# First batch's q and k turned by unit-matrix products, last batch in two token parts, and a new order of work

## The chip, the cores and the metric

The kernel runs on one core of one Trainium2 chip. The metric is the device time of one execution in microseconds (us); the time before is the median of three runs.

## The reference

Two stages follow each other. All inputs are float32.

```python
# stage 1: window attention, B=8, H=8, S=576, D=64, window 32 on both sides
scores = (q @ k.T) / 8                       # per batch and head
scores = where(|i - j| <= 32, scores, -1e9)
x = softmax(scores) @ v                      # heads side by side: x is [8, 576, 512]

# stage 2: four attention experts (E=4, width 64), two chosen per token
logits = x @ w_gate                          # [8, 576, 4]
w = softmax over the two largest logits of a token
for e in range(4):
    q, k, v = x @ wq[e], x @ wk[e], x @ wv[e]
    ye = softmax(causal(q @ k.T / 8)) @ v @ wo[e]
    out += (weight of e for the token, or 0) * ye
```

## The kernel before, in words

The work is cut into short steps, and the string `ORDER` lists some nine hundred of them by name. The program is built by walking the list: every step appends its instructions to the queues of the engines that it uses, and each engine works through its own queue in that order. So the list, written out as a constant, fixes what each engine does next. A step is written as `op`, `batch`, further digits, then a letter for the engine or the queue (`a` ScalarE, `v` VectorE, `g` GpSimd; for loads `e` SyncE's queue and `f` ScalarE's queue), then `@` and the banks of PSUM. PSUM has eight banks, all in one tile `PS`; a step that writes a bank waits until the bank's last reader is done.

A load (`load`) also waits for the last TensorE instruction ahead of it in the list, and all but one of the loads and all stores of the kernel before go through the queue of SyncE. A step of TensorE that stands late in the list thus holds the loads behind it.

The steps of the window attention of a batch, where a batch's eight heads are two groups of four:

- `lq`, `lk`, `lv`: loads of q, k and v. A group's q or k is 128 rows (four heads, 32 positions each) of 18 x 64 elements; a load of part 0 is all of it, 576 KB, and parts 1 and 2 are its halves.
- `tq`, `tk` (line 292): VectorE turns 32x32 blocks, two instructions for each group and each of q and k, one for each half of the 64 elements of a head (`dh`). They give `Tqn` and `Tkn`.
- `sc` (line 177 through the helper `mm`): the scores. A batch's group has two halves of 288 columns. A half is ten blocks, five for each `dh`, each over four heads, so 40 products that contract 32 rows and accumulate over `dh`.
- `ex` (line 337): ScalarE's exponential out of PSUM, two instructions for a half. `mk` (line 341): the window mask as a product, on GpSimd or VectorE.
- `vc`: a copy of v to other partitions. `av`: probabilities times v, in five pieces of the tokens. `un` (lines 368 to 374): the division by the row sum on VectorE.
- `xt` (line 180): TensorE transposes the result; `xf` and `xb` (lines 169 and 171, the helper `copy`) bring it out of PSUM and into bf16.

The steps of the experts, where four experts are two pairs `j`: `ga`, `gt`, `ge`, `gm`, `gu` for the gate; `pp`/`pe` for the projections; `pv`/`ve` for the values; `ps`/`xe`/`se` for scores, exponential and causal mask; `po` for probabilities times values of a pair, `oe` (lines 552 to 554) for its division; then the pair is turned, by a DMA (`dt`, line 567) in batches 0 to 6 and on TensorE (`pt`, copied out by `ot`) in batch 7; `py`, `ye`, `st` for the output projection, its copy and its store.

At the start, `zz` steps run four products of a zero matrix each. Their results are never read. The constants are made by the `s_` steps; `s_pads` writes the fixed zeros and ones of several tiles on VectorE.

Of the kernel before, what the change touches and what calls it, by code (L numbers as in the profile page):

```python
# [8 lines left out]
F32 = mybir.dt.float32  # L9
# [10 lines left out]
S = 576  # L20
# [4 lines left out]
NOE = 4  # L25

ORDER = """
    s_zero s_ones lk000:e lq000:e lv03 lk012:e tk000:e lq011:f zz1@0 zz0@0 lq012:e lk011:e s_ident s_mask lq100:e
    tq000:e sc000@02 lk100:e s_warm ex0001@2 tq011:e ex0000@0 sc001@46 ex0010@4 lv01 lv02 zz4@0 tk012:e tq012:e
    tk011:e sc010@02 mk0001:g mk0000:v ex0100@0 tq100:e lv00 tk100:e ex0101@2 zz2@4 lk110:e sc011@40 ex0011@6 zz3@2  # L30
    ex0110@4 mk0011:g vc00:a lv04 s_pads lq110:e lw00 sc101@26 vc01:a mk0101:v mk0100:v lw11 ex0111@0 av01@4 un01@4
    mk0110:g mk0010:g mk0111:g av00@0 un00@0 av04@4 lw2 xt00@0 un04@4 xf00:a@0 av03@4 ex1010@2 ex1011@6 tk110:e lw01
    av02@0 lq200:e un03@4 sc100@26 lk200:e xt02@4 ex1001@6 xf02:a@4 un02@0 xt01@0 xb02:a tq110:e mk1011:g sc110@64
    ex1000@2 xb00:g cw11:g xf01:v@0 lw10 tq200:e cw01:g mk1000:g cw2:g sc111@20 ex1101@4 xb01:a cw10:g lv13 lv11
    pp011@4 ex1100@6 lwg cw00:a tk200:e pp010@6 lv12 lv10 ex1110@2 pp000@2 pe011:a@4 pe000:v@2 pp001@4 ex1111@0
    sc201@02 lq210:e pe001:v@4 pe010:a@6 ps002@6 mk1010:v ga0@4 mk1111:v mk1110:v mk1100:v lv14 mk1101:g mk1001:g
    vc10:g ex2010@0 vc11:g lk210:e gt0@4 ps001@0 xe002@6 se002 ex2011@2 xe001@0 pv00@6 sc200@20 lq300:e tq210:e
    ve00:a@6 ex2000@2 av12@6 un12@6 ex2001@0 ps011@2 xe011@2 lq310:e ge0@4 av13@0 un13@0 ps000@2 pv01@5 xe000@2 av10@6
    tk210:e ps03@0 lv21 un10@6 xt11@2 ve01:a@5 xe03@0 av11@0 xf11:a@2 lk300:e un11@0 lv22 av14@5 ps010@2 un14@5 gm0@4
    xt10@6 xf10:v@6 xe010@2 xt12@5 xf12:a@5 sc211@02 lv20 lv24 tq300:e lv23 xb12:a ex2110@0 ga1@5 gt1@5 gu0@4 sc210@60  # L40
    ex2111@2 xb11:a mk2010:g mk2000:g se010 mk2011:g xb10:g lq400:e mk2001:g pp110@2 ex2100@6 ex2101@0 pp101@6 ge1@5
    tk300:e pp111@0 pe110:a@2 pe101:a@6 vc20:a mk2111:g mk2101:g se011 lw3 lk310:e pe111:v@0 gm1@5 gu1@5 tq310:e
    mk2100:g vc21:g pp100@2 pe100:a@2 pv11@4 sc300@60 mk2110:g ex3000@6 ex3001@0 pv10@2 ve10:a@2 av21@6 lq410:e av23@0
    un21@6 av22@2 un23@0 ps101@6 un22@2 lv32 ps100@0 av24@5 cw3:g se000 mk3000:g se001 xe100@0 xe101@6 se03 un24@5
    xt21@2 lv31 xt22@5 lk400:e xf22:v@5 xf21:a@2 ve11:v@4 xb22:g ps012@0 av20@6 sc301@24 un20@6 xt20@6 xe012@0
    ex3011@4 lv33 tk310:e ex3010@2 mk3001:g xb21:g se012 xf20:a@6 po00@0 lq500:e ps13@4 ps112@2 po01@6 xe112@2 oe00@0
    xe13@4 ps102@0 xe102@0 sc311@24 oe01@6 mk3011:g mk3010:g ex3111@4 lk500:e xb20:g sc310@60 pp201@4 ex3110@2 lv30
    lk410:e ex3100@6 ex3101@0 ps111@2 ps110@6 pp200@0 pe201:a@4 tk400:e xe111@2 lv34 pp211@4 tq400:e pp210@2 xe110@6
    lv42 pe210:a@2 pe200:v@0 pe211:v@4 tq410:e pv20@6 ve20:a@6 sc400@02 mk3101:g mk3111:g mk3100:g vc31:g se101
    mk3110:g dt00 se100 vc30:g tk410:e dt01 ex4000@0 ex4001@2 lv40 sc401@46 ps202@0 ga2@2 ex4011@6 mk4011:g se110 se13  # L50
    mk4001:g se102 lv43 pv21@3 av33@6 lq600:e xe202@0 av30@0 ve21:a@3 ex4010@4 gt2@2 py02@3 ge2@2 ye02:a@3 lk600:e
    av32@4 gm2@2 un33@6 un30@0 av34@3 py01@6 lv41 ye01:a@6 gu2@2 un32@4 un34@3 po10@0 xt32@2 lv50 xf32:a@2 av31@4
    ps23@6 xe23@6 oe10@0 ps211@2 un31@4 xe211@2 xt31@0 ps210@6 mk4000:g xe210@6 sc411@42 xf31:v@0 lv51 lq510:e xt30@0
    ex4110@4 ex4111@2 tk500:e tq500:e xf30:a@0 sc410@64 ex4101@4 py00@2 ye00:v@2 ex4100@6 se112 xb32:g mk4010:g se111
    xb31:g ps201@0 vc41:g ps200@4 xb30:g se202 vc40:g pp301@6 xe201@0 xe200@4 pp311@0 lk510:e pe301:v@6 sc501@24
    pe311:a@0 sc500@60 ex5010@2 tq510:e lv44 pp300@2 ex5011@4 lv53 ex5000@6 pp310@4 po11@6 ex5001@0 pe300:a@2 tk600:e
    pe310:a@4 oe11@6 ps300@0 ps301@2 mk4101:g mk4110:g mk4111:g av43@4 se200 mk4100:g lk610:e pv31@6 xe300@0 av40@0
    xe301@2 av41@2 un43@4 un40@0 ve31:a@6 lv54 av42@4 un41@2 ps212@6 dt10 ps302@0 xe212@6 ga3@2 xe302@0 av44@3 un42@4
    ps33@4 xe33@4 tq600:e dt11 un44@3 st00 xt41@6 xf41:a@6 lv61 lv52 xt40@0 gt3@2 ge3@2 gm3@2 xt42@3 xf40:a@0 xf42:a@3
    sc600@46 ex6001@6 ex6000@4 mk5000:g lq610:e tk510:e mk5010:g se201 se300 se210 se302 xb41:g se212 se23 se211  # L60
    xb42:a pv30@0 gu3@2 lv63 ve30:v@0 xb40:a sc510@64 mk5011:g ex5100@6 lv64 lq710:e pp401@2 pe401:a@2 pp411@0
    pe411:a@0 po20@6 oe20@6 st02 st01 ex5101@4 py10@2 ye10:a@2 st10 sc511@04 sc601@62 ex5111@4 lk710:e ex5110@0
    ex6011@2 po21@4 ps310@0 ex6010@6 tk610:e oe21@4 tq610:e se33 ps312@2 pp410@6 xe310@0 xe312@2 vc50:g mk6000:g
    mk5100:g mk5001:g vc51:g mk5101:g pe410:a@6 se301 pp400@0 pe400:a@0 po30@4 mk5111:g se310 lq700:e ps311@2 oe30@4
# [12 lines left out]
    pp610@2 lv74 se502 pp601@4 pe610:v@2 mk7100:g po50@0 xe511@6 se511 mk7110:g ps611@2 pe601:v@4 ps602@6 xe611@2
    oe50@0 po41@4 xe602@6 oe41@4 ps610@0 av71@2 xe610@0 av70@6 un71@2 ps600@4 ps510@0 dt41 xe510@0 un70@6 av72@2
    xe600@4 av73@6 ps612@0 xe612@0 ps601@4 un72@2 av74@2 un73@6 st30 ga6@3 un74@2 ps63@6 ps512@0 xe601@4 gt6@3 xe63@6
    xt71@4 ge6@3 xe512@0 se510 se600 se612 se512 xt72@2 xf71:a@4 py31@6 gm6@3 gu6@3 se611 dt40 py40@0 xt70@4 xf72:a@2  # L80
    xb72:g ye40:a@0 xb71:g po51@2 ye31:v@6 py32@0 oe51@2 xf70:a@4 py42@1 pv71@4 pv61@5 st31 st40 py41@6 dt51 xb70:g
    se602 se63 pv60@2 ye41:a@6 ve60:v@2 se610 se601 ve71:v@4 pv70@6 ve61:a@5 dt50 po61@2 ve70:a@6 pp710@4 po60@6
    ye32:v@0 st32 oe61@2 st41 pp711@2 pe710:a@4 oe60@6 pe711:a@2 pp701@4 ye42:v@1 ps710@6 pe701:a@4 ps712@0 xe712@0
    py50@2 ye50:v@2 pp700@4 xe710@6 py51@0 pe700:a@4 ps73@6 ps711@2 xe73@6 st42 se73 se710 se712 xe711@2 ps701@4 dt60
    ye51:v@0 xe701@4 ga7@6 gt7@6 ps702@0 xe702@0 se701 ps700@2 dt61 st50 se711 py52@7 ge7@6 xe700@2 ye52:v@7 py60@4
    gm7@6 se702 po71@0 gu7@6 st51 py61@2 oe71@0 se700 po70@6 pt71@0 oe70@6 st52 ye60:a@4 ot71:v@0 st60 py62@1 pt70@4
    ot70:v@4 ye61:a@2 st61 py701@0 py710@2 ye701:v@0 py700@3 ye62:a@1 st62 st701 py72@0 ye710:v@2 py711@1 ye700:a@3
    st710 ye711:a@1 st700 st711 ye72:v@0 st72
# [559 lines left out]
```

## Time and profile before

| | us |
|---|---|
| median of 3 runs | 236.77 (235.77 to 236.83) |
| the profiled execution's own time | 235.27 |
| its span, first to last instruction | 233.5 |
| TensorE (PE) busy | 213.4 (91% of the span) |
| VectorE (DVE) busy | 180.2 (77%) |
| GpSimd (POOL) busy | 148.9 (64%) |
| ScalarE (ACT) busy | 146.3 (63%) |
| granted TensorE clock, mean | 0.995 |

Busy time is the union of an engine's instructions in the trace. Every TensorE product of float32 stands in the trace as two records, and the end of a record is modelled, so an engine that is called busy may still be waiting for a part of that time. "PEld" is TensorE's loading of the stationary matrix, which overlaps its products. An instruction's idle time before it carries the name of what released it; "issue" means that the profile shows nothing that it waited for.

### The profile page before, as it was taken

The numbers are of one execution on the slowest core, as the hardware profiler recorded it, in microseconds if no ns is written. First come the engines' busy times: TensorE is split into PE (matmuls) and PEld (weight loads), VectorE is DVE, ScalarE is ACT, GpSimd is POOL, SyncE is SP. The second block draws the span as 40 slices with busy tenths as digits, with TensorE's granted clock in tenths as the row PEclk, the third lists the DMA queues.
The fourth block names the chain that finished last, engine by engine and source line by source line (L and its number), as shares of the span: only waits on it lengthen the run. The fifth ranks groups of instructions, "written<-read, shape, count | busy, mean of one in ns | idle before, by whom it ended". The sixth has DMA issues, their size and how long they took to land.

```text
span 233.5 us, 12227 instructions
## 1 busy us (share of the span) xinstructions
PE 213.4 (91%) x5472; PEld 169.7 (73%) x5486; DVE 180.2 (77%) x354; ACT 146.3 (63%) x223; POOL 148.9 (64%) x180
## 2 busy tenths in 40 slices
PE   6497999989999999899999969999999999999970
PEld 1374877868798977786898758987788787786540
DVE  1998889999977996779889449998577477645671
ACT  2067356856756876368768558577686667746931
POOL 7028195754996876989957598398978662630500
PEclk9999999999999999999999999999999999999998
DMA  6988889867867789956669975696752016284865
GB/s 234 317 207 237 208 253 207 247 207 194 212 210 202 235 261 113 247 151 149 170 151 157 280 272 188 156 81 170 171 152 93 6 25 150 101 139 137 251 213 204
DMA packets 64549, 42.94 MB, mean 184 GB/s; under 512 B 54768, under 2 KB 55792, under 8 KB 64496
## 3 DMA queue, kind: packets, MB, share of 16 engines
q1 hardware_dynamic: 64352, 41.86, 70.0%
q8 instruction: 43, 0.70, 1.3%
q10 hardware_dynamic: 144, 0.29, 0.4%
q14 instruction: 10, 0.08, 0.1%
HBM read 30.42 MB, written 9.44 MB: 171 GB/s over the span
## 4 chain that ended last, share of the span: by engine, by line
PE 59%; DVE 19%; POOL 7%; DMA 7%; issue 5%; ACT 1%; DVEq 0%; POOLq 0%; ACTq 0%
PE PS L177 55%; DVE Tkn L292 6%; DVE Tqn L292 4%; PE PS L180 4%; DVE A L341 3%; DMA V<-in_v_dram 3%; POOL A L341 3%; POOL V L171 2%; DMA kn<-in_k_dram 2%; DVE XN L369 2%; DMA out_dram<-Y 2%; POOL XTB L171 1%; POOL ATE L517 1%; DVE XTF L171 1%; DVE RC L368 0%
## 5 line engine op out<-in xcount | busy, mean ns | idle before, releaser
L341 POOL TENSOR_TENSOR A<-A,MASKP 128x576 f32<-128x576 f32 x57 | 80.0, 1416 | 20.0 <-ACT A L337 19.6
L514 ACT ACTIVATE ATE<-PS 128x1024 bf16<-128x1024 f32 x48 | 47.3, 1024 | 16.5 <-PE PS L177 14.0
L337 ACT ACTIVATE A<-PS 128x576 f32<-128x576 f32 x64 | 38.9, 651 | 23.7 <-PE PS L177 22.7
L177 PE MATMUL PS<-Tqn,Tkn 32*64 32x128 f32 (+3 forms) x2560 | 46.4, 276 | 6.8 <-DVE Tqn L292 4.6
L177 PEld LDWEIGHTS PS<-Tqn,Tkn 32*64 32x64 f32 x2560 | 40.4, 135 | 15.2 <-DVE Tqn L292 6.3
L177 PE MATMUL PS<-V,A 128*64 128x65 f32 (+1 forms) x1280 | 40.8, 223 | 3.4 <-DVE XN L369 1.2
L177 PEld LDWEIGHTS PS<-V,A 128*64 128x64 f32 (+1 forms) x1280 | 36.9, 132 | 7.9 <-issue 3.0
L292 DVE STREAM_TRANSPOSE Tkn<-kn 128x576 f32<-128x576 f32 (+1 forms) x34 | 37.4, 1180 | 6.4 <-DMA kn<-in_k_dram 5.6
L517 POOL TENSOR_SCALAR_AFFINE_SELECT ATE<-ATE 128x256 bf16<-128x256 bf16 x64 | 25.6, 414 | 24.7 <-ACT ATE L514 20.7
L292 DVE STREAM_TRANSPOSE Tqn<-qn 128x576 f32<-128x576 f32 (+1 forms) x34 | 37.2, 1178 | 0.6 <-DMA qn<-in_q_dram 0.6
L171 POOL COPY V<-V 64x2048 f32<-64x2048 f32 (+1 forms) x12 | 21.0, 1748 | 6.3 <-DMA qn<-in_q_dram 2.8
L369 DVE TENSOR_TENSOR XN<-PS,RC 128x512 f32<-128x512 f32 x32 | 22.1, 692 | 1.2
L177 PE MATMUL PS<-WO,OTT 128*128 128x512 bf16 (+1 forms) x85 | 18.4, 342 | 1.5 <-DVE OTT L171 0.8
L180 PE MATMUL PS<-ident,XN 128*128 128x128 f32 x144 | 19.1, 278 | 0.0
L169 ACT COPY XTF<-PS 128x128 f32<-128x128 f32 (+1 forms) x23 | 13.6, 631 | 7.6 <-PE PS L180 6.9
L177 PE MATMUL PS<-XTB,WK 128*128 128x288 bf16 x128 | 17.9, 286 | 0.4 <-issue 0.3
L177 PE MATMUL PS<-WV,XTB 128*128 128x256 bf16 (+1 forms) x192 | 18.2, 256 | 0.0
L169 ACT COPY Y<-PS 128x1024 f32<-128x1024 f32 (+2 forms) x13 | 9.8, 752 | 13.2 <-PE PS L177 13.2
L177 PE MATMUL PS<-XTB,WQ 128*128 128x288 bf16 x128 | 17.9, 286 | 0.0
L169 ACT CAST QKE<-PS 128x576 bf16<-128x576 f32 x21 | 13.4, 645 | 6.8 <-PE PS L177 6.8
L177 PEld LDWEIGHTS <-ATE 128*128 128x128 bf16 x448 | 16.1, 97 | 2.0 <-issue 0.4
L171 DVE COPY Y<-PS 128x1024 f32<-128x1024 f32 (+2 forms) x13 | 11.6, 894 | 7.5 <-PE PS L177 4.4
(76 smaller groups left out, 273.0 us busy)
## 6 DMA issues: line engine op xcount, KB each, us to landing
kn<-in_k_dram SPq DMA_DIRECT2D x15, 576.0 KB, 4.8
qn<-in_q_dram SPq DMA_DIRECT2D x15, 576.0 KB, 5.1
V<-in_v_dram SPq DMA_DIRECT2D x32, 256.0 KB, 4.2
out_dram<-Y SPq DMA_DIRECT2D x14, 512.0 KB, 4.0
V<-in_v_dram SPq DMA_DIRECT2D x8, 128.0 KB, 4.6
out_dram<-Y SPq DMA_DIRECT2D x16, 64.0 KB, 2.9
out_dram<-Y SPq DMA_DIRECT2D x4, 256.0 KB, 2.6
kn<-in_k_dram SPq DMA_DIRECT2D x2, 288.0 KB, 5.7
```

The lines of the kernel that those rows point to most:

```text
L169: nc.scalar.copy(o, i)
L171: eng(c).tensor_copy(o, i)
L177: last_pe[0] = nc.tensor.matmul(*a, **kw)
L180: last_pe[0] = nc.tensor.transpose(*a)
L292: nc.vector.transpose(T[:, :].rearrange("q (p o) -> q o p", o=18)[:, o0:o1], n_[:, o0:o1, 32 * dh:32 * dh + 32])
L337: nc.scalar.activation(AT[(2 * b + g) % NAT_][half][p], two(b0)[:, :, 0:HS], EXP, scale=scale_att)
L341: eng(c).tensor_tensor(out=ap, in0=ap, in1=MASK[:, None, HS * half:HS * half + HS].to_broadcast([128, 2, HS]), op=MULT)
L369: nc.vector.tensor_tensor(out=XN[T // 2][:, T % 2, :].rearrange("p (g h d) -> p g h d", g=2, h=4), in0=u[:, :, :, 0:64], in1=rc[:, :, :, N ...
L514: nc.scalar.activation(chunk(ATE[(2 * b + j) % len(ATE)], ch), two(b0), EXP, scale=scale_moe)
L517: nc.gpsimd.affine_select(ap, ap, pattern=[[0, n], [1, w]], compare_op=IS_GE, fill=0.0, base=0, channel_multiplier=-1)
```

## The change

Three things change.

1. In batch 0 both groups' q and k are no longer turned on VectorE. New steps `hq`, `hk` and `hr` multiply 64-row slices of the loaded tile by a 64x64 unit matrix on TensorE, 32 products in `hq` and in `hk` (16 of a head's 18 slices for two halves of the partitions) and 8 in `hr` (the last two slices of q and of k). New steps `eq`, `ek` and `er` copy the results out of PSUM into `QKT`. These hold a whole head's 64 elements on 64 partitions, so `sc` of batch 0 contracts 64 rows at once: 20 products for a half where there were 40. The loads of batch 0 are no longer cut into halves.
2. In batch 7, `po`, `oe`, `pt` and `ot` of each pair are each cut in two by tokens: tiles 0 and 1, and tiles 2 to 4. One store of the last batch goes through ScalarE's queue.
3. `ORDER` is another list. Over the whole list, VectorE has 7 masks before and 10 after, of 64; of the 26 steps `ye` it has 13 before and 7 after, of the 24 steps `xf` 7 and 4, of the 32 steps `pe` 11 and 13; what leaves it goes to ScalarE, but the masks come from GpSimd. ScalarE also takes four of the six weight conversions `cw` where it had one.

```diff
-    QKT = {nm: [many(2, [128, S], F32, f"T{nm}{g}") for g in range(2)] for nm in ("qn", "kn")}
+    QKT = {nm: many(2, [128, 2, S], F32, f"T{nm}") for nm in ("qn", "kn")}
...
+    PETURN = ((0, 0), (0, 1))
+
+    def turn_rows(nm, b, g, todo):
+        n_ = NAT[nm][(2 * b + g) % NNAT]
+        for r, o, bank, at in todo:
+            s = slice(64 * r, 64 * r + 64)
+            mm(PS[s, bank, at:at + 64], n_[s, o, :], ident[s, s], start=True, stop=True, skip_group_check=True)
+
+    def turn16(nm, b, g, b0):
+        turn_rows(nm, b, g, [(r, 8 * (u ^ r) + i, b0 + (u ^ r), 64 * i)
+                             for u in range(2) for i in range(8) for r in range(2)])
...
+    def hr(c, b, g, b0):
+        for u in range(2):
+            for i in range(2):
+                for r in range(2):
+                    turn_rows(("qn", "kn")[u ^ r], b, g, [(r, 16 + i, b0 + (u ^ r), 64 * i)])
+
+    def lay(c, nm, g, src, o0, o1):
+        copy(c, QKT[nm][g][:, :, :].rearrange("q h (p o) -> q h p o", o=18)[:, :, :, o0:o1],
+             src.rearrange("q (o h p) -> q h p o", h=2, p=32))
...
     def sc(c, b, g, half, b0, b1):
...
+        if (b, g) in PETURN:
+            for par, m, dh, lo, hi in BLK[half]:
+                k0 = 128 * m + 64 * par
+                for hh in (0, 2, 1, 3) if not dh else ():
+                    r = slice(32 * (hh & 2), 32 * (hh & 2) + 64)
+                    mm(PS[64 * par:64 * par + 64, bank[hh], lo - c0:hi - c0], K[r, hh & 1, k0:k0 + 64], Q[r, hh & 1, lo:hi],
+                       start=True, stop=True, skip_group_check=True)
+            return
...
+    TPARTS = [(0, 2), (2, 5)]
...
+    def po(c, b, j, *at):
         A, V = ATE[(2 * b + j) % len(ATE)], VE[b % 2]
+        U = outs(at)
+        t0, t1 = half(at)[1:]
         for eo in range(2):
-            for qt in range(NQT):
-                o = PS[:, b0 + eo, 65 * qt:65 * qt + 65]
+            for qt in range(t0, t1):
+                o = U[:, eo, qt - t0, :]
```

The start of the list, before and after:

```
before: s_zero s_ones lk000:e lq000:e lv03 lk012:e tk000:e lq011:f zz1@0 zz0@0 lq012:e lk011:e s_ident s_mask lq100:e
        tq000:e sc000@02 lk100:e s_warm ex0001@2 tq011:e ex0000@0 sc001@46 ex0010@4 lv01 lv02 zz4@0 tk012:e tq012:e
        tk011:e sc010@02 mk0001:g mk0000:v ex0100@0 tq100:e lv00 tk100:e ex0101@2 zz2@4 lk110:e sc011@40 ...
after:  s_ident s_zero lq000:f lk000:e lk010:f s_mask zz4@0 zz0@0 lq100:e lq010:e zz1@0 hq00@0 zz2@2 s_pads s_ones lk100:e
        eq00:a@0 lv04 hr00@2 s_warm lv01 zz3@0 er00:a@2 hk00@0 hk01@2 lv02 lv00 lv03 hr01@4 ek00:v@0 sc000@60 ek01:a@2
        er01:a@4 ex0000@6 sc001@24 ex0010@2 hq01@6 tk100:e tq100:e lk110:e lq110:e eq01:a@6 sc010@26 ex0011@4 ex0001@0
        ex0101@6 mk0001:v mk0101:v mk0010:v ex0100@2 sc011@40 ex0111@0 lq200:e lwg lw01 mk0111:v mk0100:v vc01:a mk0000:g
        ex0110@4 mk0011:g vc00:g sc100@62 ex1000@6 av01@0 ...
```

The end of the list after: `... po701@6 ... po711@7 oe701@6 pt701@6 po700@2 ye60:a@0 st60 ot701:a@6 po710@3 oe711@7 pt711@4 oe700@2 py62@5 ye62:a@5 ot711:v@4 py710@2 pt700@0 ye710:a@2 py711@1 oe710@3 ot700:a@0 st62 st710 ye711:a@1 st711 pt710@3 ot710:v@3 py701@2 py700@3 ye700:v@3 ye701:a@2 py72@0 st701 ye72:a@0 st700:t st72`.

More of the change, by code (lines that the diff above doesn't have):

```diff
@@ L27 @@
 ORDER = """
[L28 to L52, printed above, removed]
@@ L83 @@
[L83 to L87, printed above, removed]
@@ L88 @@
-    st710 ye711:a@1 st700 st711 ye72:v@0 st72
+    s_ident s_zero lq000:f lk000:e lk010:f s_mask zz4@0 zz0@0 lq100:e lq010:e zz1@0 hq00@0 zz2@2 s_pads s_ones lk100:e
+    eq00:a@0 lv04 hr00@2 s_warm lv01 zz3@0 er00:a@2 hk00@0 hk01@2 lv02 lv00 lv03 hr01@4 ek00:v@0 sc000@60 ek01:a@2
+    er01:a@4 ex0000@6 sc001@24 ex0010@2 hq01@6 tk100:e tq100:e lk110:e lq110:e eq01:a@6 sc010@26 ex0011@4 ex0001@0
+    ex0101@6 mk0001:v mk0101:v mk0010:v ex0100@2 sc011@40 ex0111@0 lq200:e lwg lw01 mk0111:v mk0100:v vc01:a mk0000:g
@@ L89 @@
+    oe711@7 pt711@4 oe700@2 py62@5 ye62:a@5 ot711:v@4 py710@2 pt700@0 ye710:a@2 py711@1 oe710@3 ot700:a@0 st62 st710
+    ye711:a@1 st711 pt710@3 ot710:v@3 py701@2 py700@3 ye700:v@3 ye701:a@2 py72@0 st701 ye72:a@0 st700:t st72
 """
@@ L547, in po, with oe, pt, ot @@
                     mm(o, P[:, at:at + 128], V[:, kt, 2 * j + eo, :], start=(kt == 0), stop=(kt == qt))
-    def oe(c, b, j, b0):
-        p_ = two(b0)[:, :, 0:325].rearrange("p e (t c) -> p e t c", c=65)
-        rg, O = RG[j], OE[(2 * b + j) % NOE]
+    def oe(c, b, j, *at):
+        t0, t1 = half(at)[1:]
+        p_ = outs(at)
+        rg, O = RG[j][:, :, t0:t1], OE[(2 * b + j) % NOE]
         nc.vector.reciprocal(p_[:, :, :, 64], p_[:, :, :, 64])
-        nc.vector.tensor_tensor(out=rg, in0=p_[:, :, :, 64], in1=GG[b % 2][:, 2 * j:2 * j + 2, :], op=MULT)
-        nc.vector.tensor_tensor(out=O[:, :, :, :].rearrange("p t e d -> p e t d"), in0=p_[:, :, :, 0:64],
-                                in1=rg[:, :, :, None].to_broadcast([128, 2, NQT, 64]), op=MULT)
-    def pt(c, b, j, b0):
+        nc.vector.tensor_tensor(out=rg, in0=p_[:, :, :, 64], in1=GG[b % 2][:, 2 * j:2 * j + 2, t0:t1], op=MULT)
+        nc.vector.tensor_tensor(out=O[:, t0:t1, :, :].rearrange("p t e d -> p e t d"), in0=p_[:, :, :, 0:64],
+                                in1=rg[:, :, :, None].to_broadcast([128, 2, t1 - t0, 64]), op=MULT)
+    def pt(c, b, j, *at):
+        b0, t0, t1 = half(at)
         o = one(b0).bitcast(BF16)
         O = OE[(2 * b + j) % NOE]
-        for t in range(NQT):
-            turn_pe(o[:, 128 * t:128 * t + 128], O[:, t, :, :].rearrange("p e d -> p (e d)"), ident_bf)
-    def ot(c, b, j, b0):
-        copy(c, OTT[b % 2][:, j, 0:S], one(b0).bitcast(BF16)[:, 0:S])
+        for t in range(t0, t1):
+            turn_pe(o[:, 128 * (t - t0):128 * (t - t0) + 128], O[:, t, :, :].rearrange("p e d -> p (e d)"), ident_bf)
+    def ot(c, b, j, *at):
+        b0, t0, t1 = half(at)
+        n = min(128 * t1, S) - 128 * t0
+        copy(c, OTT[b % 2][:, j, 128 * t0:128 * t0 + n], one(b0).bitcast(BF16)[:, 0:n])
     def dt(c, b, j):
```

116 lines of the change are left out of this document (80 added, 36 removed).

## The prediction

> **What bounds the kernel now.** I read the page's busy shares first, then its chain, then the windows by stage, then the time line of the start and of the end.
>
> ```profile
> PE 213.4 (91%) x5472; PEld 169.7 (73%) x5486; DVE 180.2 (77%) x354; ACT 146.3 (63%) x223; POOL 148.9 (64%) x180
> PE 59%; DVE 19%; POOL 7%; DMA 7%; issue 5%; ACT 1%; DVEq 0%; POOLq 0%; ACTq 0%
> ```
>
> TensorE is busy for 213.4 of 233.5 us, but the chain puts 19% on VectorE, so there are stages with another limit. The windows show which (columns: stretch, its length, then busy time and instructions of PE, PEld, DVE, ACT and POOL, granted clock, DMA share, GB/s):
>
> ```profile
> 0.00:8.77 8.77, 3.60 (x9) 1.04 (x9) 3.98 (x7) 1.49 (x2) 4.62 (x15) 1.00 0.81 266
> 8.77:18.00 9.23, 8.88 (x327) 6.84 (x330) 9.23 (x14) 3.58 (x6) 1.88 (x2) 1.00 0.84 238
> 18.00:23.80 5.80, 4.25 (x124) 2.95 (x126) 4.59 (x23) 4.55 (x4) 4.79 (x4) 1.00 0.85 238
> 23.80:57.40 33.60, 31.64 (x910) 25.74 (x907) 32.04 (x48) 20.10 (x37) 19.12 (x18) 1.00 0.84 223
> 57.40:130.00 72.60, 71.51 (x2038) 59.78 (x2041) 62.13 (x118) 50.69 (x79) 60.22 (x69) 1.00 0.83 188
> 130.00:140.00 10.00, 7.72 (x241) 6.00 (x242) 3.85 (x7) 5.52 (x9) 7.72 (x6) 1.00 0.92 279
> 140.00:215.00 75.00, 74.51 (x1684) 60.92 (x1687) 54.48 (x119) 51.38 (x77) 47.10 (x61) 1.00 0.51 122
> 215.00:225.00 10.00, 9.13 (x145) 5.69 (x144) 7.60 (x21) 7.85 (x11) 3.47 (x9) 1.00 0.74 238
> 225.00:233.50 8.50, 2.12 (x11) 0.76 (x12) 2.27 (x4) 1.17 (x2) 0.00 (x0) 0.87 0.53 182
> ```
>
> There are three regimes. Until 18 us VectorE, which turns q and k, has no gap (9.23 of 9.23). From 23.8 to 57.4 VectorE (32.04 of 33.60) and TensorE (31.64) are both nearly full. From 57.4 to 225 TensorE sets the pace, and what it leaves idle is 1.09 + 2.28 + 0.49 + 0.87 = 4.7 us. After 225 a chain of short steps and stores ends the run. Of the work that the change adds on TensorE, whatever is not covered by waiting is paid in full later; waits that it takes away are at most those few.
>
> **The start: what is removed and added.**
>
> ```profile
> GB/s 234 317 207 237 208 253 207 247 207 194 212 210 202 235 261 113 247 151 149 170 151 157 280 272 188 156 81 170 171 152 93 6 25 150 101 139 137 251 213 204
> 1.26 3.59 PE L177 MATMUL PS<-ZERO 128*128 128x512 bf16 x8 [1.26 <-DVE ZERO L210]
> 5.29 2.34 DVE L292 STREAM_TRANSPOSE Tkn<-kn 128x576 f32<-128x576 f32 x2 [3.85 <-DMA kn<-in_k_dram]
> 8.77 0.84 PE L177 MATMUL PS<-Tqn,Tkn 32*64 32x96 f32 x16 [3.91 <-DVE Tqn L292]
> 9.84 3.58 PE L177 MATMUL PS<-Tqn,Tkn 32*64 32x96 f32 x144 [0.24 <-DVE Tqn L292]
> 13.36 1.04 PE L177 MATMUL PS<-ZERO 128*128 128x512 bf16 x3
> 13.95 0.75 DVE L341 TENSOR_TENSOR A<-A,MASKP 128x576 f32<-128x576 f32 x1
> 14.32 1.39 PE L177 MATMUL PS<-Tqn,Tkn 32*64 32x96 f32 x80
> 22.02 0.68 PE L177 MATMUL PS<-V,A 128*64 128x65 f32 x14 [1.10 <-ACT V L169]
> 23.04 1.62 PE L177 MATMUL PS<-V,A 128*64 128x65 f32 x48 [0.34 <-DVE A L341]
> 190.98 2.09 PE L177 MATMUL PS<-V,A 128*64 128x65 f32 x64
> L292 DVE STREAM_TRANSPOSE Tkn<-kn 128x576 f32<-128x576 f32 x30 | 35.0, 1244 | 6.4 <-DMA kn<-in_k_dram 5.6 <-PE PS L177 0.8
> L341 DVE TENSOR_TENSOR A<-A,MASKP 128x576 f32<-128x576 f32 x7 | 8.9, 1310 | 0.0
> L337 ACT ACTIVATE A<-PS 128x576 f32<-128x576 f32 x64 | 38.9, 651 | 23.7 <-PE PS L177 22.7 <-issue 0.7
> L169 ACT COPY XTF<-PS 128x1024 f32<-128x1024 f32 x11 | 11.2, 1017 | 6.9 <-PE PS L180 6.9
> L171 DVE COPY Y<-PS 128x1024 f32<-128x1024 f32 x7 | 8.5, 1221 | 6.1 <-PE PS L177 3.7 <-ACT QKE L169 1.8 <-ACT A L337 0.6
> L169 ACT COPY V<-V 64x2048 f32<-64x2048 f32 x1 | 1.9, 1896 | 0.0
> ```
>
> Removed from VectorE: batch 0's turning, two groups by q and k by two instructions, 8 x 1.24 = 9.9 us by the whole-tile row (halved instructions make about the same sum). One copy `ek00` comes back, 1.22 us.
>
> Added on TensorE: `hq` and `hk` twice each and `hr` twice. No product of 64 rows by 64 columns in float32 stands in the trace. The nearest row is `av` at 190.98: 64 records of 65 columns, on two separate column strips of the array, in 2.09 us. An `hq` is also 64 records, of 64 columns, alternating between two corners of the array; I take 2.0 us, and 0.5 us for `hr` with its 16 records. If the two corners did not run side by side it would be 4.0; if more overlapped, 1.0. Together 4 x 2.0 + 2 x 0.5 = 9.0 us (4.5 to 18).
>
> Scores of batch 0: 40 records in place of 80 over twice the rows; the 80 take 1.39 us. Half is 0.7; four places in the array where there were eight could make 1.9. I take 1.2, so four steps save 0.8 us.
>
> Rate of TensorE: before, the first 160 score records (8.77 and 9.84) take 4.4 us, the later 80 (14.32) take 1.39, so the early ones run at some 60% of the later rate: TensorE had waited 3.91 us. Likewise eight zero products take 3.59 us at 1.26, and four about 1.04 at 13.36. In the new list four more zero products (`zz1`) follow at once, so TensorE works from 1.26 on without that pause, and I count the turns at the later rate. The Trainium skill, "TensorE: Matmul & The Clock Gate", Part 1, says that an idle array gets half its clock and the full one after about 3.4 us of sustained work. The two rates of these rows agree; by it the turns run at full rate from the first or second on, which is what I count anyway, and it lowers the chance of the half-rate rival below.
>
> Walk through the new list, each time being start to end in us:
> - Loads: k of group 0 was there at 5.29 with 288 KB on ScalarE's queue beside it. Now 576 KB of q run beside it; 288 KB more at 317 GB/s are 0.9 us, so both at about 6.2. `zz1` ends between 5.9 and 6.6.
> - `hq00` 6.4-8.4, `zz2` to 9.4, `hr00` to 9.9. `zz3` writes bank 0, which `eq00` (ScalarE, 1.02) reads until 9.5, so it costs only itself: to 10.9. `hk00` to 12.9, `hk01` to 14.9, `hr01` to 15.4.
> - `ek00` on VectorE 13.0-14.2; `sc000` 15.4-16.6. `ek01` and `er01` on ScalarE 15.0-16.6; `sc001` 16.7-17.9. `ex0000` to 17.4 frees banks 6 and 7; `hq01` 17.9-19.9.
> - `eq01` 20.0-21.0, with TensorE waiting 1.2 us: `sc010` 21.1-22.3. ScalarE runs `ex0011` and `ex0001` 21.0-22.3 (0.65 each); `sc011` 22.4-23.6; `ex0101`, `ex0100`, `ex0111` to 24.4; `vc01` 1.90, to 26.3; `sc100` 23.8-25.2.
> - VectorE, which has run the pads early and `tk100`, `tq100` by 19, starts the five masks ahead of `av01` at 22.4. At 0.9 each (0.75 alone, 1.31 the mean of the seven) they end at 26.9 (26.2 to 29.0). `av01` 27.0-28.0; TensorE has waited 1.8 us for it.
>
> Before, `av01` has its 32 records split between 22.02 and 23.04 and ends at about 23.8, with five score steps of two batches behind it. After, it ends at 28.0 with five behind it as well. The start is 4.2 us later. The queue that is passed is SyncE's: `lv02`, `lv00`, `lv03` are held until `hk01` (14.9) and land about 5 us later, still ahead of `vc01` at 24.4, so they cost nothing unless they slip by over 4 us.
>
> **Until 57 us.** The waits of TensorE between 23.8 and 57.4 are 33.60 - 31.64 = 1.96 us; these are what the delay can be made good from. VectorE, equal with TensorE here, is nearer its own place than TensorE is: two more masks (2 x 1.31) are behind it. I count half of the waits as regained: 4.2 - 1.0 = +3.2 us at the point that was 57.4 (2.2 to 4.2).
>
> **57 to 225.** The products are the same. VectorE gives six `ye` and three `xf` to ScalarE, 3 x 1.22 and up to 6 x 1.22 us; neither engine is full (62.13 and 50.69 of 72.60), so this costs and brings nothing of itself. The longest wait is this one:
>
> ```profile
> 137.44 1.29 PE L177 MATMUL PS<-Tqn,Tkn 32*64 32x128 f32 x70 [1.93 <-issue]
> ```
>
> It lies in the middle of a score step and no engine released it. A new order of loads moves it or ends it, and can put another one elsewhere. I leave the 4.7 us of waits as they are, 0 (none left) to 9 (twice as many).
>
> **The end.**
>
> ```profile
> 222.87 0.19 PE L177 MATMUL PS<-VE,AT 128*128 128x65 bf16 x1
> 223.57 0.83 DVE L554 TENSOR_TENSOR OE<-PS,RG 128x640 bf16<-128x640 f32 x1
> 224.45 0.45 PE L180 MATMUL PS<-ident_bf,OE 128*128 128x128 bf16 x5 [0.68 <-DVE OE L554]
> 225.01 0.46 DVE L171 COPY OTT<-PS 128x576 bf16<-128x576 bf16 x1 [0.25 <-PE PS L180]
> 225.75 2.12 PE L177 MATMUL PS<-WO,OTT 128*128 128x512 bf16 x11 [0.85 <-DVE OTT L171]
> 228.19 0.42 DVE L171 COPY Y<-PS 128x256 f32<-128x256 f32 x1 [0.17 <-issue]
> 229.58 1.53 SPq L598 DMA_DIRECT2D out_dram<-Y  x2
> ```
>
> Before, the last product of `po` ends at 223.06 and the span 10.4 us later: division, turn (0.45), copy (0.46), output products (2.12), copies, two stores in SyncE's queue (1.53) and 2.4 us from the last issue's end, 231.11. After, the last `po` piece has two tiles of five. Its division waits behind that of `po700`, two of about 0.8 us (0.33 for the product, the rest for the short ones ahead of it); a turn of 0.2, a copy of 0.25, four output products of 0.26, two copies (0.6 and 0.4), three issues in SyncE's queue (one fewer than before, 2.2 in all) and 2.4 make 8.6 with the handovers. So 1.8 us less; because the products still queued beside it (`py62`, `py710`, `py711`) can hold it, I take 1.5 (0 to 1.9).
>
> **The sum.** +3.2 at 57 us, 0 in the middle, -1.5 at the end: +1.7. The profiled execution's 235.27 is its span plus 1.8 around it, and lies 1.5 below the median of the runs; it would become 237.0, and the median 236.77 becomes **238.5 us**, 0.7% slower. A measurement of this kernel can tell about 0.5%, 1.2 us, from no change.
>
> **The rivals.**
> - *Faster, the long queue of TensorE loses its waits.* For it: the windows leave 4.7 us idle in 167, half of it in ten us beside a DMA share of 0.92; a list with loads placed otherwise need not meet that. Against: the wait has no releaser that a list could move. If the waits of 75 to 100, 130 to 140 and 215 to 225 go, about 1.0 + 2.3 + 0.9 less 0.5 that stays, and the end gives all 1.9: 3.2 - 3.7 - 1.9 = -2.4, so 234.4. It decides once more than 3 us of waits go.
> - *No change, the stage to 57 us follows VectorE.* VectorE is 95% busy there. At `av01` it is 4.2 late but 2.6 ahead in masks, so 1.6 late. If it alone sets that stage, TensorE is 1.6 late at its end too, and -1.5 at the end leaves +0.1: 236.9. Against: TensorE is 94% busy in the same stretch.
> - *Much slower, the turns run at the early rate.* If TensorE keeps the rate of the 9.84 row until 12.6 as before, `hq00` to `hk00` stretch by half of 6.2 us: +3.1 on top of +1.7, 241.6. It decides if `hq00` takes over 3.5 us. For it: the zero products before it ran slowly, and a late q lets TensorE pause. Against: the pause is under 1 us by the walk, where it was 3.9.
> - The turns are real products and VectorE's are gone from the list, so that nothing happens at all is no case.
>
> **How the numbers follow.** Forecast 0.38, faster rival 0.30, no change 0.20, half rate 0.12. The forecast's own range is 237.2 to 240, by the bounds of the stage to 57 us and of the end. The range leaves out a tenth on each side: below, the part of the faster rival in which all the waits go, so 233.4; above, the worse part of the half-rate case, so 241.6. Faster by over 0.5%: 0.31. Within: 0.20 and a small part of the forecast, less the tails of the others, 0.21. Slower: 0.48.
>
> **What would show it.** In the profile after: `hq00` at 6.4 us with 64 records in 2.0 us; `av01` ending near 28.0 rather than 23.8; a TensorE idle time of about 5 us between 57 and 225; and about 8.6 us between the last `po` product and the end. The forecast is wrong if `av01` ends before 26 us, if the turns take under 1.3 us or over 3 each, or if the middle's waits fall under 2 us or rise over 8.

## The result, and the profile after

The changed kernel takes 243.45 us (median of four runs, 242.21 to 245.36), the kernel before on the same chip 236.8 us (235.77 to 237.1). The ratio is 1.035, 95% interval 1.028 to 1.041: 3.5% slower. The profiled execution took 243.06 us with a span of 240.9, 7.4 us longer than before's 233.5. The forecast of 238.5 had the sign and not the size, and its range ended at 241.6. Some executions of every kernel are over 1.5% slower than its fastest: a median here and below takes them in and a ratio leaves them out, so the two can differ. A helper's line numbers differ by a few between the kernels (L177, L176 and L174 are all `mm`).

From the page after, busy shares and the chain by engine:

```profile
PE 221.3 (92%) x5614; PEld 176.5 (73%) x5614; DVE 169.2 (70%) x346; ACT 160.0 (66%) x241; POOL 139.2 (58%) x174
PE 83%; issue 5%; ACT 4%; DVE 3%; DMA 2%; SPq 0%; ACTq 0%; DVEq 0%
```

VectorE's 19% of the chain have become 3%: the change does what it is for. The chain is TensorE's now, and 5% of it is "issue", time with no releaser (5% before as well). The time line of TensorE at the start (start, length, operation, count, wait before it):

```profile
6.49 2.15 PE L177 MATMUL PS<-ident,qn 64*64 64x64 f32 x64
11.12 3.95 PE L177 MATMUL PS<-ident,kn 64*64 64x64 f32 x128
20.72 3.96 PE L177 MATMUL PS<-Tqn,Tkn 64*64 64x96 f32 x160 [1.12 <-ACT Tqn L169]
25.89 0.65 PE L177 MATMUL PS<-V,A 128*64 128x65 f32 x14 [0.94 <-ACT V L169]
27.32 1.86 PE L177 MATMUL PS<-V,A 128*64 128x65 f32 x56 [0.79 <-DVE A L388]
```

This is the walk of the prediction nearly row for row: `hq00` from 6.49, 64 records in 2.15 us, a wait of 1.12 for `eq01`, then in `av01` 0.94 us for the copy of v and 0.79 for the masks, 1.7 in all for the walk's 1.8. The last product of `av01` ends at 28.1 us, where before it ended at 23.8: 4.3 us late. Then after does not regain; it loses. When the two executions are laid beside each other at equal counts of products, after is 3 to 4.3 us late until 44 us, and 5 to 7.7 from 48 to 68, 6.5 at the point that was 57.4. (The lists order the products differently, so such a count wanders by about 1 us.) The stage that follows the start in after (here 28.30 to 64.20, for before's 23.80 to 57.40, with 18 more weight loads than there; 28.10 to 63.90 has as many and the same idle time) and a part of the rest, by windows (columns as in the prediction):

```profile
28.30:64.20 35.90, 31.09 (x928) 25.79 (x925) 31.08 (x54) 23.80 (x35) 15.04 (x20) 1.00 0.74 200
64.20:228.00 163.80, 159.63 (x4028) 128.46 (x4014) 118.61 (x245) 119.23 (x179) 113.00 (x137) 1.00 0.64 158
```

TensorE is idle 35.90 - 31.09 = 4.81 us in that stage, where it was 1.96. VectorE and ScalarE have room in it (31.08 and 23.80 of 35.90). So what ends the waits? First before, then after, from the view of waits over the whole span (total us, times, longest):

```profile
PE PS L177 <- issue: 3.1, 4, 1.9
```

```profile
PE PS L177 <- issue: 6.3, 8, 1.5
```

In the stage itself before has none of them (its four end at 94 us and later), after 3.3 us. Where the two longest of after stand, on TensorE's time line after:

```profile
46.75 0.24 PE L177 MATMUL PS<-V,A 128*64 128x65 f32 x1 [0.31 <-issue]
48.50 1.15 PE L177 MATMUL PS<-V,A 128*64 128x65 f32 x31 [1.51 <-issue]
50.88 1.74 PE L177 MATMUL PS<-V,A 128*64 128x65 f32 x52
54.13 0.57 PE L177 MATMUL PS<-V,A 128*64 128x65 f32 x12 [1.51 <-issue]
```

Both fall inside one step, `av`: after 1 of 32 records, and after 52 of 64. Waits of `av` for v or a mask carry a name, like the 0.79 us at 27.32 above; these two have none. The views of DMA traffic show what is. Four stretches of after, each with its packet count and queues (packets, MB, share of 16 engines), in the order 40.7 to 46.1, 46.1 to 47.1, 47.1 to 51.7 and 51.7 to 52.7 us:

```profile
DMA packets 3021, 1.31 MB, mean 243 GB/s; under 512 B 2893, under 2 KB 2893, under 8 KB 3021
q1 hardware_dynamic: 3021, 1.31, 101.8%
...
DMA packets 864, 0.24 MB, mean 236 GB/s; under 512 B 863, under 2 KB 863, under 8 KB 863
q1 hardware_dynamic: 863, 0.22, 119.5%
q8 instruction: 1, 0.02, 5.9%
...
DMA packets 603, 1.17 MB, mean 255 GB/s; under 512 B 367, under 2 KB 367, under 8 KB 603
q1 hardware_dynamic: 603, 1.17, 78.6%
...
DMA packets 35, 0.11 MB, mean 109 GB/s; under 512 B 14, under 2 KB 14, under 8 KB 34
q1 hardware_dynamic: 34, 0.09, 23.0%
q8 instruction: 1, 0.02, 5.6%
```

The queue q8 carries instructions. No packet of it moves for over 5 us (the one before landed at 40.60), then one at 46.13 to 47.08, and TensorE resumes at 48.50; none again until the one at 51.76 to 52.65, and TensorE resumes at 54.13. The page counts 44 packets and 0.72 MB on q8, 16 KB each; TensorE's 5614 loads and 5614 products over 44 are 255 instructions for each. That fits a block of 256 instructions of TensorE's own program, 128 records of products, and the theory is that TensorE stood still because the block was not there. All eight waits with no releaser in after stand at a record count of 128 n + 79 to 89, and all but the one of 0.31 end 1.24 to 1.50 us after the end of a packet. Before's wait at 135.50 (shown in the prediction) is one too: its packet ends at 135.97, TensorE resumes at 137.44.

### The profile page after: what moved, and what is told of

Its sections match the earlier page's. It is cut to its first block, busy times and chain, and to the rows that moved or that the text cites. A ratio compares the mean times of both kernels' runs of the same rounds, so it can differ in the third digit from the quotient of the medians.

```text
span 240.9 us, 12502 instructions
## 1 busy us (share of the span) xinstructions
PE 221.3 (92%) x5614; PEld 176.5 (73%) x5614; DVE 169.2 (70%) x346; ACT 160.0 (66%) x241; POOL 139.2 (58%) x174
## 4 chain that ended last, share of the span: by engine, by line
PE 83%; issue 5%; ACT 4%; DVE 3%; DMA 2%; SPq 0%; ACTq 0%; DVEq 0%
PE PS L177 77%; PE PS L180 6%; DMA Y<-in_moe_wq_dram 2%; DVE XN L416 1%; ACT A L384 1%; ACT Y L169 1%; ACT XTF L169 0%; ACT XTB L169 0%; ACT Tqn L169 0%; DVE OE L617 0%; ACT VE L169 0%; ACT ATE L561 0%; DVE RC L415 0%; SPq L183 0%; ACT WQ L169 0%
## 5 line engine op out<-in xcount | busy, mean ns | idle before, releaser
L388 POOL TENSOR_TENSOR A<-A,MASKP 128x576 f32<-128x576 f32 x54 | 76.2, 1427 | 34.2 <-ACT A L384 31.7
L177 PE MATMUL PS<-Tqn,Tkn 32*64 32x128 f32 (+7 forms) x2400 | 44.4, 269 | 3.9 <-issue 2.2
L177 PEld LDWEIGHTS PS<-Tqn,Tkn 32*64 32x64 f32 (+1 forms) x2400 | 39.2, 131 | 9.5 <-issue 5.3
L177 PE MATMUL PS<-V,A 128*64 128x65 f32 (+1 forms) x1280 | 39.9, 223 | 5.9 <-issue 3.3
L177 PEld LDWEIGHTS PS<-V,A 128*64 128x64 f32 (+1 forms) x1280 | 36.2, 132 | 11.0 <-issue 6.8
L292 DVE STREAM_TRANSPOSE Tkn<-kn 128x576 f32<-128x576 f32 x28 | 32.5, 1243 | 3.8 <-PE PS L177 3.3
L292 DVE STREAM_TRANSPOSE Tqn<-qn 128x576 f32<-128x576 f32 x28 | 32.4, 1240 | 0.6 <-PE PS L177 0.3
L416 DVE TENSOR_TENSOR XN<-PS,RC 128x512 f32<-128x512 f32 x32 | 22.1, 691 | 1.1
L171 POOL COPY V<-V 64x1536 f32<-64x1536 f32 (+1 forms) x11 | 18.3, 1667 | 3.8 <-DMA V<-in_v_dram 3.6
L169 ACT COPY Y<-PS 128x1024 f32<-128x1024 f32 (+2 forms) x19 | 13.9, 747 | 9.2 <-PE PS L177 5.6
L177 PE MATMUL PS<-WO,OTT 128*128 128x512 bf16 (+1 forms) x96 | 19.7, 347 | 0.4 <-ACT OTT L169 0.3
L169 ACT COPY XTF<-PS 128x1024 f32<-128x1024 f32 (+1 forms) x25 | 17.1, 726 | 3.7 <-PE PS L180 3.1
L171 POOL CAST XTB<-XTF 128x128 bf16<-128x128 f32 (+1 forms) x20 | 12.8, 663 | 11.0 <-DVE XTF L171 6.1
L177 PE MATMUL PS<-WV,XTB 128*128 128x256 bf16 (+1 forms) x192 | 18.5, 256 | 0.2 <-DVE G L495 0.2
L177 PE MATMUL PS<-XTB,WQ 128*128 128x288 bf16 x128 | 17.9, 287 | 0.8 <-ACT A L384 0.8
L177 PE MATMUL PS<-XTB,WK 128*128 128x288 bf16 x128 | 17.9, 287 | 0.3 <-ACT A L384 0.3
L177 PE MATMUL PS<-QKE 64*128 64x64 bf16 (+4 forms) x192 | 17.2, 278 | 0.7 <-issue 0.7
```

What stands on the lines that cost most here:

```text
L169: nc.scalar.copy(o, i)
L171: eng(c).tensor_copy(o, i)
L177: last_pe[0] = nc.tensor.matmul(*a, **kw)
L292: nc.vector.transpose(T.rearrange("q (p o) -> q o p", o=18)[:, o0:o1], n_[:, o0:o1, 32 * dh:32 * dh + 32])
L388: eng(c).tensor_tensor(out=ap, in0=ap, in1=MASK[:, None, HS * half:HS * half + HS].to_broadcast([128, 2, HS]), op=MULT)
L416: nc.vector.tensor_tensor(out=XN[T // 2][:, T % 2, :].rearrange("p (g h d) -> p g h d", g=2, h=4), in0=u[:, :, :, 0:64], in1=rc[:, :, :, N ...
```

## The experiments

The theory: TensorE waits for its instruction blocks; where the boundaries fall in the list, and how busy the DMA engines are, sets how much. The rivals: the new list is slower through its dependences; or only the start and the end matter.

**Moving the boundaries and nothing else.** Products of zeros, never read, go in just ahead of the first `av`, in the list as `zt9`. Each is four instructions (two loads, two products), so 16 move all later boundaries by a quarter of a block. Variants differ in the count alone, 16, 32, 48 or 64, and in the kernel they are put into.

```diff
+    def zt(c, n, b0):
+        Z = ZERO[:, :].bitcast(F32)
+        for i in range(16):
+            r = slice(64 * (i % 2), 64 * (i % 2) + 64)
+            mm(PS[r, b0, 0:64], Z[r, 0:64], Z[r, 64:128], start=True, stop=True, skip_group_check=True)
-    ... ex1000@6 av01@0 av00@4 ...
+    ... ex1000@6 zt9@0 av01@0 av00@4 ...
```

After, by a quarter: 

> The changed kernel with 16 zero products (64 instructions of TensorE) ahead of the first av, where TensorE waits anyway. Theory A says that the waits of 1.5 us at 47 and 53 us stand where a block of 256 instructions ends and the next has not come: they move 64 instructions forward in the work, so they stand in front of the gate's or other products 32 records earlier, not in front of the same av products; the sum of such waits may change by 2 us either way, 241.5 to 245.5. A rival (av waits there for a mask or for v): the waits stay in front of the same av products, 243.5 to 244.

After, by a half: 

> After, with 32 products of zeros (64x64, float32, 32 of about 0.033 us, 1.1 us) ahead of the first product of weights and v, which is 128 instructions of TensorE: half of one of the 16 KB blocks of 256 in which its instructions are fetched. Block theory: every block boundary behind the start falls 64 records earlier in the list; the waits of about 1.5 us leave the steps they stand at in after (47, 53, 77, 105, 142 us) and stand at others, their sum is neither that of after nor that of the shift by 64; the time is at least 3 us away from 243.4 plus 1.1. Rival, the list of orders alone sets the time: 243.4 to 244.5, waits at the steps where after has them.

Before, by a quarter, as the control: 

> Control: the kernel before, nothing else changed, with 16 products of zeros (64 instructions of TensorE, 0.5 us) ahead of the first product of weights and v. Block theory: the two long waits of before (93.8 and 135.5 us, with no releaser) move to other steps, others of 0.7 to 2.9 us appear, and the time is at least 3 us from 236.8, most likely above (240 to 250), though before's list was never touched. Rival, the new list is what is bad: before stays at 236.8 to 237.5.

After, by a whole block: 

> After, with 64 products of zeros ahead of the first product of weights and v: 256 instructions of TensorE, one whole block. Block theory: every boundary behind the start falls on the same steps as in after, so the waits stand where after has them (first product of v after the scores at about 48 and 54 us) and the time is that of after plus at most the products' own 2.1 us: 243.5 to 245.6. Rival, any work put in at the start unsettles the list: 255 or more, as with a quarter (257.2) and a half (260.3) of this.

After, by three quarters: 

> After, with 48 products of zeros (192 instructions, three quarters of a block) ahead of the first product of weights and v. If the place of the boundaries sets the time and after's own place is a good one for its list: 250 to 262, like the quarter and the half. If the places are good and bad by chance: anywhere from 238 to 262, and one that beats 243.4 less is as likely as not. If 64 and 128 were costly for another reason that grows with the number of products put in: above 260 here, against 245.1 of the whole block.

Before, by a half: 

> Before, with 32 products of zeros (half a block, 1.1 us) ahead of the first product of weights and v. If before's own place of the boundaries is a good one for its list: 241 to 255, above the 238 that the products alone would make; by chance alone it may fall to 233 to 235, and would then beat both kernels.

Before, by three quarters: 

> Before, with 48 products of zeros (three quarters of a block, 1.6 us). As with the half: 241 to 255 if before's own place is a good one for its list, 233 to 235 where it was one by chance among others.

The times come from several chips; each ratio is to the kernel before on the same chip.

| shift, instructions | after: us | ratio to before unshifted | before: us | ratio |
|---|---|---|---|---|
| 0 | 243.45 | 1.035 (1.028 to 1.041) | 236.8 | 1 |
| 64 | 257.17 | 1.088 (1.080 to 1.096) | 243.34 | 1.026 (1.015 to 1.036) |
| 128 | 260.26 | 1.106 (1.097 to 1.115) | 248.98 | 1.060 (1.050 to 1.071) |
| 192 | 248.34 | 1.064 (1.056 to 1.071) | 245.04 | 1.045 (1.035 to 1.055) |
| 256 | 245.05 | 1.026 (1.018 to 1.035) | | |

A quarter of a block of idle products costs after some 13 us by the ratios and before 6; a whole block, four times the work, costs 1.6 by the medians and nothing by the ratios. The waits move as told, but the expectation for the quarter, 241.5 to 245.5, missed the size of their effect. After shifted by 64 on TensorE's time line, the longest of its 12.5 us of waits with no releaser:

```profile
39.72 1.04 PE L177 MATMUL PS<-Tqn,Tkn 32*64 32x160 f32 x50
43.66 0.69 PE L177 MATMUL PS<-Tqn,Tkn 32*64 32x128 f32 x12 [2.90 <-issue]
```

After shifted by 256:

```profile
24.70 1.96 PE L177 MATMUL PS<-ZERO 64*64 64x64 f32 x58
26.90 2.31 PE L177 MATMUL PS<-ZERO 64*64 64x64 f32 x70 [0.24 <-issue]
48.80 0.24 PE L177 MATMUL PS<-V,A 128*64 128x65 f32 x1 [0.35 <-issue]
49.30 1.15 PE L177 MATMUL PS<-V,A 128*64 128x65 f32 x31 [0.25 <-issue]
55.53 0.57 PE L177 MATMUL PS<-V,A 128*64 128x65 f32 x12 [2.11 <-issue]
```

With a quarter the longest wait stands in a score step at 41 us, where after had none; with a whole block they are back at the same records of the same steps (1 and 31, 12 left). The 64 products stand as 128 records and 4.2 us, twice what the expectation counted, of which some 2 fill waits for v and the masks. The three quarters of after came out just under its 250 to 262. None of the other places is better than its own for either list, so no place of after among those tried, in steps of a quarter, beats before: the rival by which after's place is one unlucky one falls.

The waits are only part of what a moved boundary costs. After shifted by 64 has 6.2 us more of them than after, but its TensorE is also busy for 229.1 us, not 221.3, with 32 more records. The granted clock by 40 slices of the span, first after, then after shifted by 64:

```profile
PEclk9999999999999999999999999999999999999998
PEclk9999798699999997999998899999999999999999
```

In the shifted kernel the clock was 0.50 for 17 us in four stretches of 3.4 or 6.8 us; three of them, from 42.9, 97.5 and 138.5 us, begin between 0.8 us before and 1.4 us after the end of a long wait. After has none between 6.7 and 238.8 us; its own waits of 1.5 us brought none. How much of the 7.8 us of busy time the clock explains was not measured by itself.

**What makes a block late.** First a small test, two batches' v loads left out, then all loads of q, k and v behind batch 1 (the later batches then work on data that is already in the tiles).

```diff
-    ... lv22 ... lv23 ... lv21 lv20 ... lv24 ... lv30 ... lv34 ... lv31 ... lv32 ... lv33 ...
+    ...
```

> After, without the ten loads of v of batches 2 and 3 (their attention runs on the v of batches 0 and 1 that stands in the tiles). No instruction of TensorE is removed, so block boundaries stay. Theory, a block's fetch is late because it stands behind loads in the DMA engines: the waits at 47.0 and 52.6 us (1.5 us each) shrink below 0.5, the time falls by 2 to 4 us, to about 240. Rival, the fetch comes late of itself (its own request is late, whatever the loads do): both waits stay at 1.5 and the time at 243.

Measured: 240.83 us, ratio 1.022 (1.013 to 1.032). The median fell by the 2 to 4 us of the theory, though the ratio's interval overlaps that of after, and the two waits stayed in its trace (0.95 and 1.78 us): from 46 to 60 us the DMA engines still move 210 GB/s there, loads of q and k among them. This is inconclusive, hence the larger cut, in three kernels:

```diff
-    ... every lq, lk, lv of batches 2 to 7
+    ...
```

After: 

> After, without all loads of q, k and v of batches 2 to 7 (54 loads; these batches run on the data of batches 0 and 1). No instruction of TensorE goes, so blocks fall as in after. Theory, a block comes late because its packet stands behind loads: the waits with no releaser behind 40 us, some 6 us in after, sink under 1.5 us; the time is 237 or less. Rival, the block comes late of itself: at least 4 of the 6 us stay and the time is above 241.

After, shifted by a half block as well: 

> The kernel of e10_no_loads with 32 products of zeros (half a block) ahead of the first product of weights and v, the shift that with loads made 260.3. Theory, late behind loads: the place of the boundaries costs little when the DMA engines are free, at most 2 us over e10_no_loads (1.1 of it the products). Rival, late of itself: 10 us or more over e10_no_loads, as with loads.

Before: 

> Before, without the same 54 loads. Theory: its two long waits with no releaser (0.7 and 1.9 us) go: 233 to 235; after without loads is then 2 to 4 us above it, which is what the new start costs alone (4.4 us at the first product of weights and v) less what is made good. Rival: before stays at 236 to 237, and after without loads 6 to 7 above it as with loads.

Measured: 234.11 us (ratio 0.989, 0.984 to 0.994), 246.09 (1.037, 1.029 to 1.044) and 233.24 (0.983, 0.978 to 0.988). After without loads, the view of waits:

```profile
PE PS L174 <- issue: 0.9, 1, 0.9
```

The 6.3 us are 0.9, and before has no such row left. Set beside after at equal products, the kernel without loads gains 2.2 us between after's 42 and 51 us, 1.7 to 59, 0.9 from 72 to 79, 1.3 from 104 to 111 and 0.5 from 124 to 130, the places of the block waits: 6.6 of the 7.7 us that it leads by when the products end. After is now 0.9 us above before by the medians and 1.5 by the ratios, not 6.7; the expectation was 2 to 4. But the rival has a part: shifted by a half, the same kernel loses 12 us with the loads gone, as the rival expected, and not the 2 us of the theory. One of its waits:

```profile
128.61 2.52 PE L174 MATMUL PS<-Tqn,Tkn 32*64 32x64 f32 x155
132.50 0.33 PE L174 MATMUL PS<-Tqn,Tkn 32*64 32x64 f32 x5 [1.37 <-issue]
```

Here 155 score records pass in 2.52 us, so a block of 128 of them lasts about 2.1. From 128.9 to 130.9 us the DMA engines carry one packet, that of the instructions. By the count of records it started 0.83 us after the block was entered, took 1.14 us, and the next record came 1.57 us after its end: 3.5 us with nothing in the way. (The longest wait of this kernel, 2.20 us ending at 191.12, is no such clean case: the DMA engines were busy with a store and a turn of `OTT` there.) So two things make the waits: blocks that hold little but short products, which the place of the boundaries decides, and packets that come late while loads run. By the count of records, an estimate, the next packet started 4.2 and 3.3 us after the block was entered at the two long waits of after, and 1.1 and 1.0 us at the same records without loads.

**The start by itself.** After's list with batch 0 turned on VectorE again, and before's list with after's start in place of its own.

```diff
-    PETURN = ((0, 0), (0, 1))
+    PETURN = ()
-    ... hq00 zz2 hr00 zz3 hk00 hk01 hr01 ek00 ... eq00 ... hq01 ... eq01 ...
+    ... tk000 tq000 ... tk010 tq010 ...
```

> The changed kernel with its new list, but batch 0's q and k turned on VectorE again and scored in 32-row products. Theory A (the start costs about 4 us, and waits of TensorE for its own instructions cost the rest): q and k of both groups are turned one behind the other from 6.2 us, the first av starts at about 24.8 instead of 27.3, and nothing else changes: 144 products fewer and 80 more are 256 instructions of TensorE less, so what lies behind keeps its place in blocks of 256. Some 2.5 us less than the changed kernel, 241. Theory B (the loss lies in the order of the new list behind the start, and what the start loses is made good there): within 0.7 us of the changed kernel.

```diff
-    s_zero s_ones ... (before's list to its first batch's last exponential)
+    s_zero s_ones ... (after's list to the same point, hq to eq01 included)
```

> The list of before from the masks of batch 0 on, with only the new start ahead of it: batch 0's q and k turned by unit-matrix products. Theory A: av of batch 0 starts about 4 us later than in the kernel before and nothing makes it good: 240 to 242 against 236.8. Theory B: the old list makes most of it good by 57 us: 237 to 238.5.

Measured: 241.94 us (ratio 1.024, 1.015 to 1.033) and 241.38 (1.019, 1.010 to 1.027). Both are near what theory A expected, but neither gives a clean price of the start: their waits with no releaser are, in this order,

```profile
PE PS L176 <- issue: 9.3, 9, 2.8
```

```profile
PE PS L176 <- issue: 6.2, 6, 2.2
```

With the turning on VectorE, TensorE is freed of products, but inside the 32-row score steps 1.3 and 2.8 us of waits come up at 16 and 21 us, at counts where a block ends, and the granted clock was 0.50 from 11.8 to 22.1 us and again from 25.5 to 28.9: `av01` ends at 27.6, where after has it at 28.1. After's start in front of before's list raises the block waits from before's 2.9 us to 4.4; the other 1.8 of the 6.2 is one wait ahead of `av01` that ends 5.7 us after the last packet, and its cause stays open. The clock of that execution was 0.50 from 26.2 to 33.0 us.

**The end by itself.** Before with the two-part end.

```diff
-    ... se702 po71@0 gu7@6 st51 py61@2 oe71@0 se700 po70@6 pt71@0 oe70@6 ...
+    ... se702 po711@0 gu7@6 st51 py61@2 oe711@0 se700 po701@6 oe701@6 po710@1 pt711@0 ...
```

> The kernel before with only its end changed: batch 7's po, oe, pt and ot in two token parts, one store in ScalarE's queue. Theory A: the end was 0.6 us shorter in the changed kernel (9.8 us from the last po product to the end against 10.4), so 236.2. The prediction's term of -1.5 would be 235.3. No gain at all, 236.8, if SyncE's queue of stores sets the end.

In this first form `ye710`, which waits for a store, stood ahead of `ot700` in ScalarE's queue and held TensorE for 3.5 us, a fault of that order: 239.42 us, ratio 1.001 (0.995 to 1.007). Again with the two exchanged:

```diff
-    ot710:v@0 py711@1 ye710:a@4 pt700@2 st62 ot700:a@2 st710
+    ot710:v@0 py711@1 pt700@2 ot700:a@2 ye710:a@4 st62 st710
```

> The kernel before with the two-part end alone, with the copy ot700 ahead of ye710 in ScalarE's queue, so that it does not stand behind the wait for a store (3.5 us of TensorE before in e3_end_alone). Prediction's term for the end: 1.5 us less than before, 235.3 (ratio 0.994). Rival, the end waits for the stores of Y: within 0.5 us of before.

Measured: 236.97 us, ratio 1.003 (0.998 to 1.009). The predicted 0.994 is outside the interval; the rival holds. The last copies and stores of its time line:

```profile
228.72 1.38 PE L176 MATMUL PS<-WO,OTT 128*128 128x512 bf16 x8 [0.46 <-ACT OTT L168]
230.82 1.35 ACT L168 COPY Y<-PS 128x512 f32<-128x512 f32 x3 [2.15 <-DMA out_dram<-Y]
231.21 1.29 DVE L170 COPY Y<-PS 128x512 f32<-128x512 f32 x2 [3.17 <-DMA out_dram<-Y]
232.88 1.64 SPq L663 DMA_DIRECT2D out_dram<-Y  x2
```

TensorE is done 4.5 us after its last `po` product, where before it took 4.8, but the copies then stand for the stores of earlier pieces of Y, 2.15 and 3.17 us.

## Why the prediction was wrong, step by step

- **The start, +4.2: right.** +4.3 measured, by the walk's own rows, so that the sign of the forecast was no luck. `hq` took 2.15 us for 2.0, so the half-rate rival fell at once.
- **Until 57 us, +3.2 (2.2 to 4.2): the step that failed.** It is +6.5 there. The step took the 1.96 us of TensorE's waits as slack from which the delay is made good. Idle rose to 4.81 instead, 3.3 of it in the two `av` steps above. Without loads after is about 3.2 us behind before, also without loads, at the start, and about 2.2 at that point: the regaining of 1 us that the step counted on does exist, and block waits lie on top. The bound was worked from dependences, and nothing in it allowed a wait that belongs to none. The rival of no change falls with it: VectorE, which should set this stage, is busy for 31.08 of 35.90 us.
- **57 to 225, 0 (none left to twice as many): about right.** TensorE's idle is 4.9 us in the stretch that answers to it (64.2 to 232.9), for the 4.7 predicted. By the last product of `po`, which ends 8.0 us later than before, after loses another 1.5 us there; as the idle time is the same, block waits don't explain it, and its cause stays open. The prediction quoted before's 1.93 us wait, said that no engine released it, and that a new list would move it. That was the clue, applied to the wrong stretch alone.
- **The end, -1.5 (0 to -1.9): too much.** From the last `po` product to the end is 9.8 us, before 10.4, predicted 8.6: -0.6, inside its bounds; alone it is worth nothing that can be measured. On the time line after:

```profile
230.54 0.53 PE L177 MATMUL PS<-VE,ATE 128*128 128x65 bf16 x12
231.69 0.34 PE L180 MATMUL PS<-ident_bf,OE 128*128 128x128 bf16 x3 [0.62 <-DVE OE L617]
234.02 1.38 PE L177 MATMUL PS<-WO,OTT 128*128 128x512 bf16 x8 [0.30 <-ACT OTT L169]
234.08 2.30 SPq L668 DMA_DIRECT2D out_dram<-Y  x3
236.47 1.24 SPq L664 DMA_DIRECT2D out_dram<-Y  x2
```

From the end of the last `po` product, 231.07, to the start of the last output products are 2.95 us for divisions, turn and copy, where the walk had 2.05. Those products take 1.38 us, not 4 x 0.26; the issues in SyncE's queue take 2.30 + 1.24 = 3.5, not 2.2, but most of that passes beside products and copies; and from the last issue's end, 237.71, to 240.9 are 3.2 us, not 2.4. The walk's own terms also add up to 8.7 before any handover, not 8.6 with them.

With +4.3, +2.2 until 57 us (for -1.0), +1.5 in the middle and -0.6 the span is 7.4 longer; the forecast had 1.7, and 3.2 of the difference is the one step. The range of the forecast itself was too narrow by its own bounds, which give 237.1 to 241.0 and not 237.2 to 240; the range that was stated, to 241.6, stops short all the same.

The Trainium skill, "Runtime: NRT & Kernel Launch", section "Instruction fetch mechanics", says that an engine's program is refilled in 16 KiB blocks of 256 instructions while the current one runs, and that crossing a boundary is mostly hidden. Block and size agree with the 44 packets of 16 KB here; the hiding does not hold for these short products, 6.3 us in after and up to 18.2 us with the boundaries moved by 128 instructions.

## What to carry to other kernels

A wait with no releaser in the middle of a step is a term of its own: count TensorE's records to it, modulo 128, and look at the instruction packets beside it before treating idle time as slack. In the case with nothing in the way, 3.5 us passed from one block's entry to the next, so here a block of 128 records that lasts less ends in a wait (an estimate from that one case). Every edit that adds or removes TensorE instructions shifts all the blocks behind it, and one that moves loads changes when their packets come, so such an edit is best judged with its list tuned again at the new place, or at a shift of a whole block. An end that is cut finer frees the engine, not the stores behind it.

## What the runs showed of the hardware that was not expected

TensorE's next record comes 1.2 to 1.7 us after its instruction packet has landed, in nearly every wait of this kind, in after and in the kernels with moved boundaries. 64 instructions of idle products cost some 13 us in one list and 6 in another, 256 cost 1.6 at most. Even with nothing else on the DMA engines, a block of some 2.1 us of short products was too short for the next one to arrive. Around the end of about half of the waits of 1.6 us and more, in all runs, the granted clock went to 0.50 for 3.4 or 6.8 us: it was so behind the 2.90 us of after shifted by 64 and not behind before's 1.93.
